# Attention with two MoE layers on one core: other places for the first tables, the first item's weights and the first loads, and a ring with two more places

## The chip, the cores and the metric

One core of a Trainium2 chip runs the whole kernel. The metric is the device time of one execution in microseconds; the times before are three executions, with their median, and one more execution was profiled. Engines are named as the profile names them: PE (TensorE matmuls), PEld (its weight loads), DVE (VectorE), ACT (ScalarE), POOL (GpSimd) and SP (SyncE, which here issues nearly all transfers). An engine works through its instructions in the order of the program; so does each queue of transfer issues.

## The reference, cut to what matters

```python
# attention: 4 batches, 12 heads, 448 tokens, head size 64, float32
scores = cap * tanh((q @ k.T / 8) / cap)
x = softmax(scores) @ v                    # becomes 1792 tokens x 768
# hard MoE: 8 experts, each 768 -> 1024 -> 768
logits = x @ w_gate + modality_bias[modality_id]
e_idx, gate = argmax(logits), softmax(logits)[e_idx]
for e in range(8):                         # tokens with e_idx == e
    y[mask] = gate[mask] * (relu(x[mask] @ w1[e]) @ w2[e])
# soft MoE: 8 experts with 4 slots each
d, c = softmax(y @ phi, axis=0), softmax(y @ phi, axis=1)
slots = d.T @ y                            # 32 slots x 768
out = c @ concat(relu(slots[e] @ m2_w1[e]) @ m2_w2[e] for e in range(8))
```

## The kernel before

**Attention** runs over 24 pairs of heads (`NPAIR`, 6 pairs a batch, numbered 0 to 23, `LAST` = 23). The loop of `attention` (lines 693 to 731) is a software pipeline written out by hand: in the round of pair p it issues the loads of pair p+2 (`load_qkv`), the scores and the tanh and exp of pair p (`scores1`, `scores2`, `scores3`), the product with V of pair p-1 (`pv`, `pv2`, and `post1`, which copies the result `o_ps` out of PSUM), the splitting of q and k of pair p+1 into a high and a low part (`split`), and the sums, turns and scaling of pair p-2 (`post2`, `post3`; `post3` ends in a write of x to `x_dram` by SP). Three places in a round, `route(p, 0)` to `route(p, 2)`, take further work from a list that `plan` fills.

**Routing** is such work. `route_batch` ranks the tokens of a batch by expert. After the third batch, `route_first` chooses the first item: a list of 4 x 117 tokens of one expert. Its parts are `f0` and `f1` (DVE), `sums_` (12 matmuls into `tab_ps`, L329, and a copy, L332), `rest` (six small DVE instructions, among them the expert's number `et_i`) and `turn` (a matmul into `tabt_ps`, L336, and four DVE instructions that give the indices `idx` and the gates `gsl`). Then `gather` (L470) fetches the 4 x 117 rows of x by indirect transfers of POOL, and `weights_first` reads the expert's number on SP and loads the first pieces of its w1 (`rw`). PSUM is lent: `Lent.tile` hands out the bank `s0` of the scores' pool, while `sums_` uses the small pool `ps_m`.

**The items.** An item is the hard MoE of up to 468 tokens of one expert: 16 pieces of w1, each split by ACT (`wh`, L810) and DVE or POOL (`wl`), then three matmul passes (L857 to L859). `item_start` (L1100) closes the attention's pools of q, k and scores, places the items' buffers and loads four tiles `w2r` (`w2load`), which the products `wphi_ps` (L834) of the first piece read. Four items run one after the other. Ahead of the first, behind the loop of pairs (lines 733 to 748), the gathered rows are scaled by their gates (`xscale`, in turn on DVE and ACT), the first two weight pieces are split (`wfirst`) and x is transposed (`xprep`).

**The soft MoE** ends the kernel. Its weights are 64 units of 768 KB (`m2_load`, L230), all loaded by SP: 32 for layer 1, then 32 for layer 2. They go through a list of places: `NRING` = 3 places of their own at first, 12 places in the attention's arena, 5 more after it, and 12 that come free behind the last item, two of them (`ring3`) closed again by `late_start` before layer 2; then places are used again (`more`). Attention loads `NRING` + 1 units, one at every second pair from pair 4 on (lines 696 to 698); the items load 16, and the rest is loaded in the last stage. The buffers `cT` and `oT` take the room of `ring3`.

**The start** (lines 1132 to 1144): the load of `cap` by ACT, a tanh that makes ACT load its table, the loads of pair 0 and `NWARM` = 5 matmuls on zeros. `early_consts` makes a scale from `cap`, `split_qk` makes the parts of q (DVE) and k (ACT casts, DVE subtracts).

Of the kernel before, what the change touches and what calls it, by code (L numbers as in the profile page):

```python
# [10 lines left out]
F32R = mybir.dt.float32r  # L11
# [41 lines left out]
def attn_moe_softmoe(ctx, tc, qT, kT, vP, cap, modality, w_gate, mod_bias, w1, w2, w2t, phi, m2_w1, m2_w2, out):  # L53
    nc = tc.nc
# [507 lines left out]
    def weights_first():  # L562
        e_first.append(load_e(NI + 3))
        for s in range(NRW):
            wload("A", s, e_first[-1])

    def attention(a1, a1q, a2p, first, ps_s, ps_o, ps_x, ps_m, item_start):
# [94 lines left out]
        extra[9] = zero_c  # L662
        class Lent:

            @staticmethod
            def tile(shape, dt, tag, name):
                n = math.prod(shape[1:])
                a = "abcd"[:len(shape) - 1]
                t = ps_s.tile([128, 512], dt, tag="s0", name=name)[:shape[0], :n]
                return t.rearrange(f"p ({' '.join(a)}) -> p {' '.join(a)}", **dict(zip(a, shape[1:])))  # L670

        todo = {}

        def plan(b):

            p, rb = (b + 1) * NP_ + 1, route_batch(b, a2p, Lent)
            at = [(p, 2), (p + 1, 1), (p + 1, 2), (p + 2, 1)]
            if b == NB1 - 1:
                f0, f1, rest, sums_, turn = route_first(a2p, ps_m, Lent)
                rb += [f0, f1, sums_, rest, lambda: (turn(), gather(NA, NB1 * S), weights_first())]  # L680
                at += [(p + 1, 2), (p + 2, 2), (p + 3, 0), (p + 3, 0), (p + 3, 1)]
                assert p + 4 == LAST
            for k, f in zip(at, rb, strict=True):
                todo.setdefault(k, []).append(f)
# [45 lines left out]
                plan((p - 2) // NP_)  # L730
            route(p, 2)
        assert not todo and n2 == NRING + 1 and a1.end <= UNIT * (NRINGA - 1)
        wsplits, xpreps = item_start()
        pv(LAST, lambda: post3(LAST - 2, a1, ps_m))
        for i in range(NT):
            xscale(NA, bool(i % 2), i)
        adds2(LAST)
# [12 lines left out]
    def load_qkv(a1, a1q, p, eng=None):  # L750
        b, hp = divmod(p, NP_)
        qr = a1q.tile([128, S], F32, tag="qr", name="qr", bufs=2)
        kr = a1q.tile([128, S + KL], F32, tag="kr", name="kr", bufs=2)
        vt = a1.tile([128, NKC + 1, 2 * HD], F32, tag="vt", name="vt", bufs=4)
        (eng or nc.sync).dma_start(kr, kT[b, hp])
        nc.sync.dma_start(qr, qT[b, hp].rearrange("h d s -> (h d) s"))
        nc.sync.dma_start(vt, vP[b, hp])
        return qr, kr, vt

# [62 lines left out]
    def w2load(j, e):  # L822
        src = w2t[bass.ds(e, 1), :, D * j:D * j + D] if j < NP2 else w2[bass.ds(e, 1), 128 * (j - NP2):128 * (j - NP2) + 128, :]
        nc.sync.dma_start(big["w2r"][j % NR2], src.rearrange("a p f -> (a p) f"))
# [269 lines left out]
    with ExitStack() as st:  # L1094
        ps_o = st.enter_context(tc.tile_pool(name="ps_o", bufs=1, space=PSUM, side="right"))
        stq = ExitStack()
        a1q = stq.enter_context(tc.tile_pool(name="a1q", bufs=1, reuse_waits="tile"))
        ps_s = stq.enter_context(tc.tile_pool(name="ps_s", bufs=1, space=PSUM))

        def item_start():  # L1100
            stq.close()
            ps_m.pools.append(stM.enter_context(tc.tile_pool(name="ps_m2", bufs=1, space=PSUM)))
            fx = stM.enter_context(tc.tile_pool(name="b_fx", bufs=1, reuse_waits="tile"))
            ps_a = stM.enter_context(tc.tile_pool(name="b_ps_a", bufs=2, space=PSUM, reuse_waits="tile"))
            ps_t = stM.enter_context(tc.tile_pool(name="b_ps_t", bufs=1, space=PSUM, reuse_waits="tile"))
            ps_l = stM.enter_context(tc.tile_pool(name="b_ps_l", bufs=1, space=PSUM, reuse_waits="tile"))
            big.update({("ps", "a"): ps_a, ("ps", "t"): ps_t, ("ps", "x"): ps_x, ("ps", "sm"): ps_m})
            big["lp"] = ps_l.tile([R, W], F32, tag="l", name="l_ps")
            fixed = fixed_in(fx)

            x0 = [fixed([128, 3, G], n, F32R) for n in ("xh0", "xl0")]
            w_at = {}
            for i in range(NWH):
                j = (HB * (TSURE + 1) - NWH + i) % NWH
                w_at[j] = [fixed([128, WC], f"{n}{j}", F32R) for n in ("wh", "wl")]
            whs.extend(w_at[i][0] for i in range(NWH))
            wls.extend(w_at[i][1] for i in range(NWH))
            x1 = [fixed([128, 3, G], n, F32R) for n in ("xh1", "xl1")]
            for n, a, b in zip(("xh", "xl"), x0, x1):
                big[n] = [t[:, k] for t in (a, b) for k in range(3)]  # L1120
            big["h"] = [fixed([128, G], f"h{i}") for i in range(NHB)]
            big["htok"] = fixed([128, NT, NF * 128], "htok")
            big["w2r"] = [fixed([128, D], f"w2r{i}") for i in range(NR2)]
            for n in ("wphi", "dhT"):
                big[n] = fixed([128, 2, 128], n)

            big["mid"] = {"dacc": big["htok"][:, NT - 1, 128 * NF - FQ:], "wacc": fixed([128, FQ], "wmid")}
            for j in range(NR2):
                w2load(j, e_first[-1])
            return [call(wfirst, s) for s in range(AHEAD)], [call(xprep, k, "aat"[k % 3]) for k in range(KD)]  # L1130

        nc.scalar.dma_start(capt, cap.partition_broadcast(128))
        nc.vector.memset(bigf, 0.0)
        nc.vector.memset(xg_all[:, 0, :256], 0.0)
        nc.scalar.activation(out=bigf, in_=bigf, func=AF.Tanh)
        first = {0: load_qkv(a1, a1q, 0, nc.gpsimd)}

        warm = ps_o.tile([128, S], F32, tag="o", name="warm")
        for _ in range(NWARM):
            nc.tensor.matmul(warm[:, :256], lhsT=xg_all[:, 0, :128], rhs=xg_all[:, 0, :256], start=True, stop=True)  # L1140
        early_consts()
        first_split = split_qk(a1q, *first[0][:2], act=True)
        first[1] = load_qkv(a1, a1q, 1)
        attention(a1, a1q, a2p, first, ps_s, ps_o, ps_x, ps_m, item_start)

# [162 lines left out]
    with ExitStack() as st:  # L1308
# [23 lines left out]
        m2_again += range(len(m2_slots) + len(r2))  # L1332
        m2_slots += r2 + r3
        NTOT = len(m2_slots)
        assert NTOT <= 4 * E
        last, freed = {s: s for s in m2_again}, {}
        for i in range(NTOT, NW):
            s = m2_again[(i - NTOT) % len(m2_again)]
# [17 lines left out]

        def late_start():

            st3.close()
            sth.close()  # L1360
            late["f"] = pool("c_ps_f", 4, space=PSUM, reuse_waits="tile")
            fixed = fixed_in(pool("c_fx2", 1, reuse_waits="tile"))
            late["cT"] = fixed([96, NTT, 128], "cT", F32R)
            late["oT"] = fixed([96, H2], "oT", F32R)

            spare.extend(m2_slots[s] for s in sorted(m2_again, key=last.get) if last[s] >= 4 * E)
            late["ct"] = [spare[0][:, NTT * NSLOT * i:NTT * NSLOT * (i + 1)].rearrange("p (t s) -> p t s", s=NSLOT)
                          for i in range(NCD)]
            late["part"] = spare[1][:, :H2]
            late["cr"] = spare[1][:, H2:H2 + 4 * 3 * NSLOT].rearrange("p (i r s) -> p i r s", r=3, s=NSLOT)  # L1370
# [34 lines left out]
        def turn(e):  # L1405
            h = hs.pop(e)
            tp = ps_t.tile([128, 2, 128], F32, tag="t", name="hT_ps")
            for i in range(2):
                nc.tensor.transpose(tp[:, i], h[:, 128 * i:128 * i + 128], ident)  # L1409
            n = NSLOT // E  # L1410
            nc.vector.tensor_copy(hT.rearrange("p (j h) s -> p h j s", h=2)[:, :, :, n * e:n * e + n],
                                  tp.rearrange("p h (j s) -> p h j s", s=NSLOT)[:, :, :, n * e:n * e + n])

        def c_load():
            for i in range(NCD):
# [69 lines left out]
        for e in range(E):  # L1485
            layer2(0, e)
            more(4 * E + 2 * e + 2)
            if e == 4:
                c_load()
        slot_out(0)  # L1490
# [20 lines left out]
        15], "pb": [6, 7, 9, 10, 12, 13, 15], "N": [6, 6, 6, 9, 9, 9, 9, 12], "comb": 6, "gath": 0, "cur": 12, "xp": [13, 13, 13], "xs": [1, 4, 4, 12], "rest": [1, 3, 7,  # L1511
        9], "pool": [4, 5]},
}
NRING = 3
NWARM = 5
NRINGA = 12
NRINGB = 5
NRING2 = 9
# [41 lines left out]
def _build(arrays):  # L1560
    import numpy as _np
    import concourse.bacc as _bacc

    nc = _bacc.Bacc("TRN2", target_bir_lowering=False, num_devices=1)
    args = []
    for name, a in arrays.items():
        args.append(nc.dram_tensor(f"in_{name}_dram", a.shape, mybir.dt.from_np(a.dtype), kind="ExternalInput").ap())
    for i, (shape, dtype) in enumerate(_OUTS):
        args.append(nc.dram_tensor(f"out_{i}_dram", shape, mybir.dt.from_np(_np.dtype(dtype)), kind="ExternalOutput").ap())
    with tile.TileContext(nc) as tc:  # L1570
        attn_moe_softmoe(tc, *args)
    return nc
# [9 lines left out]
```

## Time and profile before

| | us |
|---|---|
| median of 3 runs (501.41, 503.65, 504.35) | 503.65 |
| the profiled execution | 503.55 |
| its span, first to last instruction | 501.8 |
| PE busy | 461.4 (92%) |
| DVE busy | 291.0 (58%) |
| ACT busy | 248.7 (50%) |
| POOL busy | 66.7 (13%) |
| transfers | 124.97 MB, mean 249 GB/s |

A row of the timeline gives the start, the busy time, engine, line and operation of one instruction or of several merged ones (their count stands behind x), and in brackets the time that the engine had been idle before it, with what ended that. A row of the windows table gives, for a stretch of time, how long each engine was busy in it and with how many instructions, the clock that TensorE was granted (1.00 is 2.4 GHz, 0.50 is 1.2 GHz), the share of time in which the 16 DMA engines were busy, and what they moved. A busy PE is not a PE at its peak.

### The profile page before, as it was taken

How to read it: one execution, taken by the hardware profiler on the slowest of the kernel's cores; microseconds unless marked ns; L12 is line 12 of the kernel's file. 1: busy time of each engine (PE TensorE's matmuls, PEld its weight loads, DVE VectorE, ACT ScalarE, POOL GpSimd, SP SyncE). 2: the span in 40 equal slices, each digit the busy share in tenths (PEclk: the TensorE clock that was granted, in tenths of full speed). 3: DMA queues.
4: the chain of work that ended last, by engine and by line, in shares of the span. 5: the costliest groups of instructions: out<-in, count | busy, mean ns of one | idle time of the engine just before them, and what ended most of it. 6: DMA issues, size and time to landing. Idle time of an engine off the chain costs nothing. (4 is left out here: it accounts for less than half of the span.)

```text
span 501.8 us, 10684 instructions
## 1 busy us (share of the span) xinstructions
PE 461.4 (92%) x4077; PEld 298.2 (59%) x4077; DVE 291.0 (58%) x738; ACT 248.7 (50%) x400; POOL 66.7 (13%) x141
## 2 busy tenths in 40 slices
PE   6999999999999979899999999999999979977673
PEld 4555555555555634678876888778877845521322
DVE  3799999999999964657552546245513332001323
ACT  4988878788798748423342335334432321100312
POOL 3000000000000003013522213121013003120000
PEclk8899999999999979899999999999999999995986
DMA  6347654653353427399959997989688899999997
GB/s 187 116 93 218 197 165 118 221 158 110 126 159 104 135 82 216 99 298 325 268 183 293 319 289 242 308 287 313 206 287 320 314 418 414 414 412 415 416 414 301
DMA packets 56151, 124.97 MB, mean 249 GB/s; under 512 B 9385, under 2 KB 25456, under 8 KB 56096
## 3 DMA queue, kind: packets, MB, share of 16 engines
q1 hardware_dynamic: 53696, 117.54, 68.0%
q0 software_dynamic: 2256, 6.71, 5.0%
q8 instruction: 33, 0.54, 0.4%
q14 instruction: 22, 0.18, 0.1%
q10 hardware_dynamic: 144, 0.00, 0.0%
HBM read 112.52 MB, written 11.71 MB: 248 GB/s over the span
## 5 line engine op out<-in xcount | busy, mean ns | idle before, releaser
L608 ACT ACTIVATE arena<-arena,capb 128x1792 f32<-128x1792 f32 (+1 forms) x48 | 77.0, 1604 | 1.6
L857 PE MATMUL acc_ps<-xh,wh 128*128 128x468 f32 x192 | 75.8, 395 | 1.3 <-DVEq L1257 0.9
L107 DVE TENSOR_TENSOR arena<-arena 128x896 f32<-128x896 f32 (+1 forms) x74 | 68.0, 919 | 13.2 <-ACT arena L608 11.4
L858 PE MATMUL acc_ps<-xl,wh 128*128 128x468 f32 x192 | 71.9, 374 | 0.0
L859 PE MATMUL acc_ps<-xh,wl 128*128 128x468 f32 x192 | 71.9, 374 | 0.0
L107 DVE TENSOR_TENSOR wl<-rw,wh 128x384 fp32r<-128x384 f32 x49 | 27.3, 559 | 71.6 <-ACT wh L810 63.1
L649 PE MATMUL o_ps<-arena 128*64 128x448 f32 x288 | 61.9, 565 | 0.4 <-DVE arena L657 0.3
L810 ACT CAST wh<-rw 128x384 fp32r<-128x384 f32 x64 | 32.3, 508 | 52.1 <-PE acc_ps L858 22.5
L605 ACT ACTIVATE arena<-s_ps 128x448 f32<-128x448 f32 x96 | 46.7, 540 | 11.3 <-PE s_ps L577 11.3
L470 POOL DMA_INDIRECT xg<-x_dram,idx x16 | 16.7, 1044 | 202.2 <-PE rt_ps L520 173.4
L857 PEld LDWEIGHTS acc_ps<-xh,wh 128*128 128x128 f32 x192 | 36.3, 189 | 6.8 <-issue 1.4
L978 ACT ACTIVATE h<-acc_ps 128x468 f32<-128x468 f32 x32 | 17.9, 561 | 42.6 <-PE acc_ps L859 39.3
L859 PEld LDWEIGHTS acc_ps<-xh,wl 128*128 128x128 f32 x192 | 36.0, 188 | 5.1 <-DVE wl L107 0.5
L858 PEld LDWEIGHTS acc_ps<-xl,wh 128*128 128x128 f32 x192 | 36.4, 189 | 3.5
L649 PEld LDWEIGHTS o_ps<-arena 128*64 128x64 f32 x288 | 18.9, 140 | 30.8 <-issue 20.9
L577 PE MATMUL s_ps<-qh,kh 64*128 64x448 f32 x144 | 32.8, 443 | 2.4 <-ACT kh L765 1.9
L577 PE MATMUL s_ps<-qh,kl 64*128 64x448 f32 x144 | 27.6, 374 | 0.1
L577 PE MATMUL s_ps<-ql,kh 64*128 64x448 f32 x144 | 27.4, 371 | 0.0
L107 POOL TENSOR_TENSOR wl<-rw,wh 128x384 fp32r<-128x384 f32 x15 | 15.6, 1040 | 74.5 <-ACT wh L810 69.0
L577 PEld LDWEIGHTS s_ps<-qh,kh 64*128 64x128 f32 x144 | 14.2, 189 | 17.7 <-ACT arena L605 8.5
L600 ACT ACTIVATE arena<-sl_ps 128x448 f32<-128x448 f32 x24 | 13.0, 543 | 23.1 <-PE sl_ps L577 22.5
L906 POOL DMA_INDIRECT c_dram<-cw,icur x16 | 16.0, 1003 | 55.4 <-DVE cw L107 42.2
(271 smaller groups left out, 756.0 us busy)
## 6 DMA issues: line engine op xcount, KB each, us to landing
ring<-in_moe_w_dram SPq DMA_DIRECT2D x30, 768.0 KB
w2r<-in_moe_w2t_dram SPq DMA_DIRECT2D x32, 384.0 KB
w2r<-in_moe_w_dram SPq DMA_DIRECT2D x28, 384.0 KB
arena<-in_moe_w_dram SPq DMA_DIRECT2D x13, 768.0 KB
rw<-in_moe_w_dram SPq DMA_DIRECT2D x24, 384.0 KB
arena<-in_moe_w_dram SPq DMA_DIRECT2D x22, 384.0 KB
arena<-in_v_dram SPq DMA_DIRECT2D x24, 256.0 KB
kr<-in_k_dram SPq DMA_DIRECT2D x23, 256.0 KB
```

What stands on the lines that cost most here:

```text
L107: (eng or nc.vector).tensor_tensor(out=out, in0=in0, in1=in1, op=op)
L470: nc.gpsimd.indirect_dma_start(out=xg[:, i, :], out_offset=None, in_=x_dram if rows is None else x_dram[:rows], in_offset=bass.IndirectOff ...
L577: nc.tensor.matmul(o, lhsT=kk[r, k], rhs=qq[r], start=(t == 0), stop=(t == 2))
L605: nc.scalar.activation(out=dst[:, h], in_=ps[h], func=AF.Tanh)
L608: nc.scalar.activation(out=t, in_=t, func=AF.Exp, scale=capb)
L649: nc.tensor.matmul(o[hd], lhsT=vt[:, c, hd], rhs=pt_t[p][:, c, h] if c < 2 else pt_m[p][:, 1 + h], start=(c == 0), stop=False)
L810: nc.scalar.copy(wh, rw)
L857: nc.tensor.matmul(ps, lhsT=wh, rhs=hi[k], start=(k == 0), stop=False)
L858: nc.tensor.matmul(ps, lhsT=wh, rhs=lo[k], start=False, stop=False)
L859: nc.tensor.matmul(ps, lhsT=wl, rhs=hi[k], start=False, stop=(k == total - 1))
L906: nc.gpsimd.indirect_dma_start(out=c_dram[i % NCD], out_offset=bass.IndirectOffsetOnAxis(ap=icur[:, i:i + 1], axis=0), in_=cw[:, i, :], in ...
L978: nc.scalar.activation(out=big["h"][n % NHB], in_=acc.pop(n), func=AF.Relu)
```

## The change

It has five parts. The first ring has five places (`NRING` = 5), taken from the scratch for descriptors of POOL's transfers, which is set to 4096 bytes of each partition; attention so loads six units, and the two places of `ring3` are closed, and `cT` and `oT` placed, behind the first expert of layer 2. In `plan`, `sums_` and `rest` of the first tables go from place 0 to place 1 of pair 22 and `turn` with the gather from place 1 to place 2; the sums use the lent bank `s0`, the turn the bank `o` of the result `o_ps`. `weights_first` leaves the gather's side and is called, together with the four loads of `w2r`, inside the last pair's `pv`, behind `post3` of pair 21. The k of pair 0 is loaded by SP and no longer by POOL, its q by ACT and no longer by SP, ahead of the tanh. The warm-up has 7 matmuls and not 5.

```diff
+            def __init__(self, pool, tag, width):
+                self.where = pool, tag, width
+            def tile(self, shape, dt, tag, name):
+                pool, tag, width = self.where
...
-                t = ps_s.tile([128, 512], dt, tag="s0", name=name)[:shape[0], :n]
+                t = pool.tile([128, width], dt, tag=tag, name=name)[:shape[0], :n]
...
+        lent_s, lent_o = Lent(ps_s, "s0", 512), Lent(ps_o, "o", S)
...
-            p, rb = (b + 1) * NP_ + 1, route_batch(b, a2p, Lent)
+            p, rb = (b + 1) * NP_ + 1, route_batch(b, a2p, lent_s)
...
-                f0, f1, rest, sums_, turn = route_first(a2p, ps_m, Lent)
-                rb += [f0, f1, sums_, rest, lambda: (turn(), gather(NA, NB1 * S), weights_first())]
-                at += [(p + 1, 2), (p + 2, 2), (p + 3, 0), (p + 3, 0), (p + 3, 1)]
+                f0, f1, rest, sums_, turn = route_first(a2p, lent_s, lent_o)
+                rb += [f0, f1, sums_, rest, lambda: (turn(), gather(NA, NB1 * S))]
+                at += [(p + 1, 2), (p + 2, 2), (p + 3, 1), (p + 3, 1), (p + 3, 2)]
...
-        wsplits, xpreps = item_start()
-        pv(LAST, lambda: post3(LAST - 2, a1, ps_m))
+        wsplits, xpreps, more_weights = item_start()
+        pv(LAST, lambda: (post3(LAST - 2, a1, ps_m), weights_first(), more_weights()))
...
-        (eng or nc.sync).dma_start(kr, kT[b, hp])
-        nc.sync.dma_start(qr, qT[b, hp].rearrange("h d s -> (h d) s"))
+        nc.sync.dma_start(kr, kT[b, hp])
+        (eng or nc.sync).dma_start(qr, qT[b, hp].rearrange("h d s -> (h d) s"))
...
-            for j in range(NR2):
-                w2load(j, e_first[-1])
-            return [call(wfirst, s) for s in range(AHEAD)], [call(xprep, k, "aat"[k % 3]) for k in range(KD)]
+            return ([call(wfirst, s) for s in range(AHEAD)], [call(xprep, k, "aat"[k % 3]) for k in range(KD)],
+                    lambda: [w2load(j, e_first[-1]) for j in range(NR2)])
...
+        first = {0: load_qkv(a1, a1q, 0, nc.scalar)}
         nc.scalar.activation(out=bigf, in_=bigf, func=AF.Tanh)
-        first = {0: load_qkv(a1, a1q, 0, nc.gpsimd)}
...
-        assert NTOT <= 4 * E
+        assert NTOT <= 4 * E + 2
...
         def late_start():
-            st3.close()
             sth.close()
             late["f"] = pool("c_ps_f", 4, space=PSUM, reuse_waits="tile")
-            fixed = fixed_in(pool("c_fx2", 1, reuse_waits="tile"))
-            late["cT"] = fixed([96, NTT, 128], "cT", F32R)
-            late["oT"] = fixed([96, H2], "oT", F32R)
...
+        def last_place():
+            st3.close()
+            fixed = fixed_in(pool("c_fx2", 1, reuse_waits="tile"))
+            late["cT"] = fixed([96, NTT, 128], "cT", F32R)
+            late["oT"] = fixed([96, H2], "oT", F32R)
...
             layer2(0, e)
             more(4 * E + 2 * e + 2)
+            if e == 0:
+                last_place()
...
-NRING = 3
-NWARM = 5
+NRING = 5
+NWARM = 7
...
-    nc = _bacc.Bacc("TRN2", target_bir_lowering=False, num_devices=1)
+    nc = _bacc.Bacc("TRN2", target_bir_lowering=False, num_devices=1, dynamic_dma_scratch_size=4096)
```

## Rows read from the trace of the kernel before

**Rows 1.** Windows: us, busy per engine, PEclk, DMA share, GB/s; the tail
```profile
413.00:440.00 27.00, 26.70 (x414) 14.26 (x418) 4.97 (x28) 3.79 (x11) 7.32 (x20) 1.00 1.02 415
...
440.00:487.10 47.10, 33.97 (x276) 11.65 (x268) 9.36 (x19) 6.61 (x14) 4.98 (x30) 0.86 1.02 414
```

**Rows 2.** Timeline of SP in the tail: start us, us, engine, line, operation, count
```profile
398.66 18.31 SPq L230 DMA_DIRECT2D ring<-in_moe_w_dram  x15
```

**Rows 3.** Timeline at the end, the last layer-2 matmuls; brackets: idle before
```profile
487.13 0.85 PE L1448 MATMUL o_ps<-ring,hE 128*32 128x384 f32 x8 [0.94 <-DMA ring<-in_moe_w_dram]
```

**Rows 4.** Timeline of the start
```profile
1.39 4.16 PE L1140 MATMUL warm<-xg 128*128 128x256 f32 x10 [1.39 <-DVE xg L1134]
...
4.88 0.15 DVE L110 TENSOR_SCALAR capb<-capt 128x1 f32<-128x1 f32 x1 [3.55 <-DMA capt<-in_cap_dram]
...
6.74 0.62 ACT L765 CAST kh<-kr 128x512 fp32r<-128x512 f32 x1 [3.93 <-DMA kr<-in_k_dram]
...
7.41 0.47 PE L577 MATMUL s_ps<-qh,kh 64*128 64x448 f32 x2 [1.86 <-ACT kh L765]
...
13.85 0.98 ACT L605 ACTIVATE arena<-s_ps 128x448 f32<-128x448 f32 x2 [0.74 <-PE s_ps L577]
```

**Rows 5.** Windows, the first scores
```profile
7.40:15.60 8.20, 7.08 (x33) 4.79 (x33) 4.24 (x10) 5.83 (x8) 1.12 (x8) 0.58 0.67 195
```

**Rows 6.** Timeline: o_ps copies of two pairs, then pair 22 on DVE and PE
```profile
34.96 0.62 DVE L657 COPY arena<-o_ps 128x448 f32<-128x448 f32 x1
...
42.43 0.62 DVE L657 COPY arena<-o_ps 128x448 f32<-128x448 f32 x1
...
176.72 0.62 DVE L657 COPY arena<-o_ps 128x448 f32<-128x448 f32 x1
...
178.22 0.25 DVE L107 TENSOR_TENSOR f_tmp<-oh,esel 112x96 f32<-112x96 f32 x1
...
179.83 1.40 PE L329 MATMUL tab_ps<-bsel,a 112*32 112x117 f32 x24 [2.77 <-DVE a L107]
...
181.29 0.28 DVE L332 COPY tab<-tab_ps 128x117 f32<-128x117 f32 x1 [1.60 <-PE tab_ps L329]
...
186.88 0.33 DVE L110 TENSOR_SCALAR arena<-r_ps,gvec 128x112 f32<-128x112 f32 x1 [1.46 <-PE r_ps L507]
...
187.56 0.16 DVE L110 TENSOR_SCALAR emp<-tabt_ps 117x4 f32<-117x4 f32 x1 [0.35 <-PE tabt_ps L336]
...
189.10 0.62 DVE L657 COPY arena<-o_ps 128x448 f32<-128x448 f32 x1
...
189.71 0.37 PE L577 MATMUL s_ps<-qh,kh 64*128 64x448 f32 x2
```

**Rows 7.** Windows, PE after the tables
```profile
181.20:187.10 5.90, 5.90 (x50) 2.30 (x48) 4.21 (x13) 0.31 (x1) 0.00 (x0) 0.61 0.41 134
```

**Rows 8.** Timeline of the handover to the first item
```profile
189.09 1.16 POOL L470 DMA_INDIRECT xg<-x_dram,idx  x1 [173.37 <-PE rt_ps L520]
...
191.24 1.94 SPq L824 DMA_DIRECT2D w2r<-in_moe_w2t_dram  x4
...
193.32 1.09 POOL L470 DMA_INDIRECT xg<-x_dram,idx  x1 [0.30 <-issue]
...
201.22 0.33 SPq L528 DMA_DIRECT2D x_dram<-arena  x1
...
203.93 0.94 ACT L478 ACTIVATE xg<-xg,gsl 117x768 f32<-117x768 f32 x1 [4.27 <-DMA xg<-x_dram,idx]
...
204.77 0.91 ACT L810 CAST wh<-rw 128x384 fp32r<-128x384 f32 x2
...
211.63 1.50 PE L834 MATMUL wphi_ps<-w2r,phi_sb 128*32 128x256 f32 x24
```

**Rows 9.** Windows, the handover's loads
```profile
191.30:198.10 6.80, 6.51 (x61) 3.17 (x59) 3.06 (x4) 6.74 (x9) 2.50 (x3) 1.00 0.97 286
```

**Rows 10.** Tile xg: the gathers' time from issue to landing
```profile
DMA to landing us min/median/max: 7.7/9.3/10.6
```

More of the change, by code (lines that the diff above doesn't have):

```diff
@@ L663, in attention @@
         class Lent:
-            @staticmethod
-            def tile(shape, dt, tag, name):
+            def __init__(self, pool, tag, width):
+                self.where = pool, tag, width
+            def tile(self, shape, dt, tag, name):
+                pool, tag, width = self.where
                 n = math.prod(shape[1:])
                 a = "abcd"[:len(shape) - 1]
-                t = ps_s.tile([128, 512], dt, tag="s0", name=name)[:shape[0], :n]
+                t = pool.tile([128, width], dt, tag=tag, name=name)[:shape[0], :n]
                 return t.rearrange(f"p ({' '.join(a)}) -> p {' '.join(a)}", **dict(zip(a, shape[1:])))
+        lent_s, lent_o = Lent(ps_s, "s0", 512), Lent(ps_o, "o", S)
         todo = {}
         def plan(b):
-            p, rb = (b + 1) * NP_ + 1, route_batch(b, a2p, Lent)
+            p, rb = (b + 1) * NP_ + 1, route_batch(b, a2p, lent_s)
             at = [(p, 2), (p + 1, 1), (p + 1, 2), (p + 2, 1)]
             if b == NB1 - 1:
-                f0, f1, rest, sums_, turn = route_first(a2p, ps_m, Lent)
-                rb += [f0, f1, sums_, rest, lambda: (turn(), gather(NA, NB1 * S), weights_first())]
-                at += [(p + 1, 2), (p + 2, 2), (p + 3, 0), (p + 3, 0), (p + 3, 1)]
+                f0, f1, rest, sums_, turn = route_first(a2p, lent_s, lent_o)
+                rb += [f0, f1, sums_, rest, lambda: (turn(), gather(NA, NB1 * S))]
+                at += [(p + 1, 2), (p + 2, 2), (p + 3, 1), (p + 3, 1), (p + 3, 2)]
                 assert p + 4 == LAST
```

## The prediction

> **What bounds the kernel now.** I read the windows table over the whole span first, then the waits of PE and SP, then the timeline where a window showed an idle or slowed PE. Three stretches are not simply "PE works".
>
> The tail is the plainest. From 413 to 440 us and from 440 to 487.1 us the DMA engines are busy all the time and move 415 and 414 GB/s [rows 1]. SP issues the weight loads of the last layer pair back to back from 398.66 us on [rows 2]. PE's last layer-2 matmuls start at 487.13 us, and they waited for a `ring` load [rows 3]. So between 398.66 and 487 us the end is set by bytes over bandwidth; what follows 487.13 is a fixed chain of outputs.
>
> The second is the start. The last load that the first scores need is k, through POOL's queue; its cast waited 3.93 us for it and started at 6.74 [rows 4]. PE has been idle for 1.86 us since its warm-up matmuls ended at 5.55 [rows 4], and between 7.4 and 15.6 us its granted clock is 0.58 [rows 5], a mixture of both levels, 1.2 GHz for most of it.
>
> The third is the handover from attention to the first item. In pair 22 PE waits 2.77 us for the tables' operand `a`, and the row of `tab_ps` shows it [rows 6]. Right after it the clock is down: 0.61 on average from 181.2 to 187.1 us [rows 7]. The o_ps copies of two undisturbed pairs stand 42.43 - 34.96 = 7.47 us apart; here it is 189.10 - 176.72 = 12.38 us [rows 6]. Then the first item waits for its inputs: the scaling of the last gathered tile starts at 203.93 after 4.27 us of waiting for the gather, and the casts of the first weights only at 204.77 [rows 8]. Everything else is a PE-bound stream, which a shift passes through unchanged.
>
> **Part 1, two more places in the first ring.** Two units of 768 KB (786,432 bytes each) move from the tail into attention, which issues one unit at every second pair, now six and not four. The total of units stays 64; the last stage has 42 and not 44 left to load. At the tail's 414 GB/s that is 2 x 0.786 MB / 414 GB/s = **3.8 us** less, all on the path that sets the end, since the engines are full over the whole of it [rows 1 to 3]. The price in attention: 1.57 MB more while it lasts. They go behind the q, k, v loads of two pairs ahead (15 us of slack at 7.47 us a pair [rows 6]), so I cost them at nothing; without that cover each would hold the next loads by 0.786 MB / 414 GB/s = 1.9 us. Freeing the last two places after layer 2's first expert rather than before it delays only the allocation of `cT` and `oT`, written several experts later: nothing. The `ct` loads keep their place. I take 3.8, between 3.4 and 4.0.
>
> **Part 2, the first loads and the warm-up.** k of pair 0 goes to SP's queue as its first load, q to ACT's behind `cap`; POOL issues nothing there. Two loads of those queues bound the landing: `cap` let DVE start at 4.88 [rows 4], and q, the first load of SP, never made DVE wait. So k is there between about 4.9 and 5.5, its cast (0.62) ends by 5.5 to 6.1, and q, now behind `cap`, comes at 5.4 to 6.0. DVE then needs 1.15 us for the high and low part of q before the low part of k, which would start at 6.6 to 7.1 and not behind the cast at 6.74 + 0.62 = 7.4 [rows 4]: a gain of 0.3 to 0.8, I take 0.5. The two extra warm-up calls are four more passes at 4.16 / 10 = 0.42 us each at most [rows 4], so PE is busy until 6.4 to 7.2 and nearly meets the first scores; they cost nothing unless the k side is ready sooner than that. Without the 1.86 us hole the clock should not fall as early. What that returns is read on ACT, which is continuous from 13.85 us on: it waited 0.74 for PE there [rows 4]. I take 0.7 of a possible 0 to 0.9. Together **1.2 us**, between 0.2 and 1.9.
>
> **Part 3, the first tables.** The sums go behind the pair's PV products and post2, and the turned table from place 1 to place 2. So PE no longer stands 2.77 us in front of PV, and the stretch at half clock behind it goes. What is late next: the turn now uses the PSUM bank of `o`, so it waits for the copy of o_ps, which is behind the whole DVE queue. DVE runs from 178.22 to the end of that copy, 189.10 + 0.62 = 189.72; in between it waited 1.60, 1.46 and 0.35 us for PE, and the 0.65 us of four table instructions (0.16 each) now come behind [rows 6]. Left are 11.50 - 3.41 - 0.6 = 7.5 us of work, so the copy ends at 185.7 to 185.9. PE, at full clock, has done its 7.5 us plus 0.7 us of sums by about 184.5, so it waits 1.2 to 1.9 us here. The last pair's scores then begin near 186.2 instead of 189.71 [rows 6]: 3.5 us sooner. The tables follow on DVE, indices at 187.3 and not 188.1; PV of pair 22, which reuses the bank, is just behind them. The gather starts about 0.8 us sooner only.
>
> **Part 4, the first item's weights.** Before, four w2r loads (1.57 MB) start at 191.24, between the four gathers, the last of which POOL issues at 193.32 [rows 8]; the engines are 0.97 busy from 191.3 to 198.1 [rows 9]. Landing took 7.7 to 10.6 us [rows 10]; the last tile was late at 203.93. Now both kinds of weight load stand on SP behind the x_dram write of post3 of pair 21 (201.22 before [rows 8], 3.5 sooner = 197.7). The gathers have the engines nearly to themselves, so I take the shortest landing: 192.5 + 7.7 = 200.2, scaling 0.94, casts at 201.1 (with the median of 9.3: 202.7). The rw loads: the write's 0.23 MB and their own 0.79 MB at the 286 GB/s of that window [rows 9] take 3.6 us, so they are there at 201.3, the first half a microsecond or more sooner. Both inputs say casts 3.6 us sooner than 204.77. Against it: w2r is now in the queue behind rw, 0.23 + 0.79 + 1.57 MB from 197.7 at 286 GB/s = 9.1 us, there at 206.8, or at 208.1 if one gather (0.36 MB) still moves beside it. The products that read it stood at 211.63 [rows 8], now 208.0. That leaves a wait of 0 to 1 us; I take 0.4. Sum of parts 3 and 4: **3.2 us**, between 0 and 4.3. Queued behind the waiting SP are the item's next loads, due several pieces later.
>
> The Trainium skill, "DMA: Bandwidth & Descriptors", section "Anatomy of one DMA — SWDGE (gpsimd) path", gives a transfer issued by GpSimd about 2.0 us plus its bytes over 436 GB/s; an estimate for a gather of 117 x 3072 bytes is 2.8 us. By it the last gather would be there at 196 and only rw would count: casts 4.0 rather than 3.6 us sooner, a time 0.4 us lower. The rows, all under load, show 7.7 or more [rows 10].
>
> **Part 5, descriptor scratch.** Nothing in the trace shows it full: POOL issues the four gathers one behind the other, with 4.2 us from the first (189.09) to the last [rows 8]. I cost it at nothing; the other end is the slow rival below.
>
> Sum on the profiled execution (503.55 us, span 501.8; the median of the runs is 503.65): 503.55 - 3.8 - 1.2 - 3.2 = **495.3 us**.
>
> **Rivals.** (a) The wait at the turn takes the place of the one removed. PE stands for 1.2 to 1.9 us; the hole of 1.86 us at the start and that of 2.77 us in this pair were each followed by half clock [rows 4 to 7]. A slowed stretch as long as the present one (5.9 us at 0.61 [rows 7]) loses 0.39 x 5.9 = 2.3 us, and with it post3 of pair 21, behind which rw stands: of the 3.2 us of parts 3 and 4 some 0.9 are left, or none if the stretch is longer. Time 497.6 to 498.5. For it: the DVE sum; against it: PE is busy up to the hole. The Trainium skill, "TensorE: Matmul & The Clock Gate", Part 1, says that the gate's window runs free of the program; by that rule a hole of this size may lower the clock in one execution and not in another, and nothing here decides it. (b) The first item is starved: w2r and the next rw share the queue with ring loads, and the wait is 3 us and not 0.4: 498. (c) The change doesn't do what it says in the tail: if PE's layer 2 and not the loads ended last, 3.8 is not won, 499.1. Against it: PE waited for loads up to the last expert [rows 3]. (d) More is won: the clock stays up at the start and over the handover, casts 4.5 sooner, start 1.9: 493.3 or less. (e) Slower: with a quarter of the scratch, POOL can't put four gathers in flight and waits until one has landed. With room for one, the fourth is issued at 188.3 + 3 x 7.7 = 211.4 and lands at 219.1, not 203.9: 15 us on the path, 513.8 us, more if the later items' gathers suffer too. With room for two, it lands at 205.1 and the time is 499.8. It decides against the change below two gathers, 234 rows. The Trainium skill's page on DMA puts the rings into the scratch of 16 partitions with 16 bytes a descriptor; an estimate from it is 256 entries per engine, far above what the 468 rows of four gathers, spread over 16 engines, would need.
>
> **How the numbers follow.** Forecast (492.5 to 497.5): 0.60. (a) 0.16, (b) 0.07, (c) 0.04, (d) below 492.5 0.07, (e) 0.06 (half of it around 500). The range reaches from 491.5, where all parts give their best, to 500.0, which takes in (a), (b) and (c). A measurement can tell about 0.5%, 2.5 us, from no change: below 501.1 lie all cases but the worse half of (e) and mishaps of several parts at once: faster 0.92, same 0.04, slower 0.04.
>
> **What would show it.** Right: SP's last-stage loads start some 4 us sooner and last 3.8 us less; PE's row of `tab_ps` without a wait and pair 22's copy 8.5 to 9 us behind the last; the last scaling near 200 us; gathers landing in under 8 us. Wrong: a clock of 0.5 after the turn; wphi_ps waiting long for w2r; gathers further than 1.4 us apart on POOL; a tail window at 415 GB/s that is as long as before.

## The result and the profile after

The changed kernel takes 497.2 us in the median of six runs (496.2 to 498.5), before 504.0 (499.8 to 506.4); the ratio is 0.9888, 95% interval 0.9851 to 0.9925, so 5.6 us less. The profiled execution took 496.8 us, its span is 495.1. That is 6.7 us under the span before. The forecast was 495.3, its range 491.5 to 500.0: right as a whole, 1.9 us under the median, with a sum whose terms did not all come out.

Where the two profiled executions part, by rows that both have (after minus before):

| row | before | after | difference |
|---|---|---|---|
| copy of o_ps, pair 21 | 176.72 | 175.07 | -1.7 |
| copy of o_ps, pair 22 | 189.10 | 183.26 | -5.8 |
| first casts of w1 | 204.77 | 199.53 | -5.2 |
| first relu of the first item | 216.43 | 212.03 | -4.4 |
| relu of item 0's third block | 277.15 | 273.17 | -4.0 |
| last relu of the items | 401.55 | 397.39 | -4.2 |
| SP's first load of the last stage | 398.66 | 394.50 | -4.2 |
| last layer-2 matmuls | 487.13 | 480.62 | -6.5 |

Item 0 is the second of the four items; the first one has no number. So the attention and the handover won 5.8 us, 1.6 of them were given back up to the last relu of the items, and the tail added 2.3. The timeline of the start of the kernel after answers to [rows 4], the window to [rows 5]:

```profile
1.38 5.32 PE L1143 MATMUL warm<-xg 128*128 128x256 f32 x14 [1.38 <-DVE xg L1137]
...
5.24 0.62 ACT L769 CAST kh<-kr 128x512 fp32r<-128x512 f32 x1 [1.96 <-DMA kr<-in_k_dram]
...
6.33 0.45 DVE L110 TENSOR_SCALAR qh<-qr,qsc 128x448 fp32r<-128x448 f32 x1 [1.06 <-DMA qr<-in_q_dram]
...
7.42 0.68 DVE L107 TENSOR_TENSOR kl<-kr,kh 128x512 fp32r<-128x512 f32 x1
...
7.00:15.60 8.60, 6.64 (x43) 3.68 (x45) 5.20 (x12) 6.86 (x9) 1.25 (x9) 1.00 0.71 209
```

k is there 1.5 us sooner, but q, behind `cap` on ACT's queue and issued at 1.30 us instead of 0.92, now makes DVE wait 1.06 us, and the low part of k starts at 7.42, as late as before. What is new is the clock: 1.00 over the first scores, where the same window before has 0.60.

The handover of the kernel after, timeline, answers to [rows 6, 8]. Its last line is the time of the first item's gathers from issue to landing:

```profile
179.63 0.81 PE L329 MATMUL tab_ps<-bsel,a 112*32 112x117 f32 x24
...
183.26 0.60 DVE L657 COPY arena<-o_ps 128x448 f32<-128x448 f32 x1
...
183.92 0.39 PE L336 MATMUL tabt_ps<-fold,tab 128*117 128x32 f32 x2 [1.01 <-DVE arena L657]
...
184.24 0.47 PE L577 MATMUL s_ps<-qh,kh 64*128 64x448 f32 x2
...
191.25 1.08 POOL L470 DMA_INDIRECT xg<-x_dram,idx  x1 [0.30 <-issue]
...
195.85 0.94 ACT L478 ACTIVATE xg<-xg,gsl 117x768 f32<-117x768 f32 x1 [1.71 <-DMA xg<-x_dram,idx]
...
196.59 0.94 SPq L552 DMA_DIRECT2D rw<-in_moe_w_dram  x2
...
199.53 0.92 ACT L814 CAST wh<-rw 128x384 fp32r<-128x384 f32 x2 [2.74 <-DMA rw<-in_moe_w_dram]
...
201.71 1.72 PE L805 MATMUL xt_ps<-ident,xg 117*128 117x117 f32 x12 [2.98 <-DVE xl L107]
...
DMA to landing us min/median/max: 4.6/4.6/4.6
```

[Rows 10] is taken over the gathers of all four items. Those of the first item alone, in the kernel before:

```profile
DMA to landing us min/median/max: 9.6/10.1/10.6
```

So these gathers land some 5 us faster now that the loads of w2r are no longer among them: from the first issue to the last landing the DMA engines are busy 0.56 of the time, before 0.84. The wait for the tables' operand is gone; PE waits 1.01 us in front of the turn. The last gathered tile is there at 195.85, and now the first weights are what ends last: issued at 196.59, cast at 199.53 after a wait of 2.74. PE has a hole of 2.98 us from that. The kernel before had a smaller one in the same place:

```profile
204.91 1.12 PE L801 MATMUL xt_ps<-ident,xg 117*128 117x117 f32 x9 [2.14 <-ACT xg L478]
```

From the first casts to the first relu, windows of the kernel before and then of the kernel after (the eighth number is PEclk):

```profile
204.77:206.77 2.00, 1.85 (x11) 1.16 (x11) 1.47 (x3) 2.00 (x6) 0.00 (x0) 0.89 0.03 8
206.77:208.77 2.00, 2.00 (x11) 1.84 (x11) 1.39 (x4) 0.80 (x2) 0.00 (x0) 0.50 0.59 186
208.77:210.77 2.00, 2.00 (x11) 1.89 (x11) 1.87 (x4) 1.10 (x2) 0.00 (x0) 0.76 0.03 11
210.77:216.43 5.66, 5.66 (x76) 4.33 (x75) 1.60 (x5) 0.52 (x2) 0.99 (x1) 1.00 0.58 148
```

```profile
199.53:201.53 2.00, 0.00 (x0) 0.00 (x0) 1.46 (x3) 2.00 (x5) 0.00 (x0) 1.00 0.88 293
201.53:203.53 2.00, 1.82 (x13) 1.29 (x13) 1.81 (x5) 1.43 (x4) 0.00 (x0) 0.99 0.96 346
203.53:205.53 2.00, 1.90 (x6) 1.65 (x6) 1.97 (x7) 0.48 (x1) 0.00 (x0) 0.50 0.99 386
205.53:212.03 6.50, 6.50 (x77) 5.00 (x76) 1.00 (x3) 0.52 (x2) 1.00 (x1) 0.89 0.65 197
```

Both kernels fall to 1.2 GHz behind their hole. Before, the way from casts to relu is 216.43 - 204.77 = 11.66 us; after, where PE stands for the first 2 us of it, 12.50. So of the 5.8 us 0.6 go before the casts and 0.8 behind them. Some 0.4 us more go in item 0, where PE's wait for w2r is longer than it was before; the rows of the kernel before and of the kernel after:

```profile
274.37 0.63 PE L834 MATMUL wphi_ps<-w2r,phi_sb 128*32 128x256 f32 x6 [0.24 <-DMA w2r<-in_moe_w2t_dram]
...
269.68 1.34 PE L838 MATMUL wphi_ps<-w2r,phi_sb 128*32 128x256 f32 x12 [0.76 <-DMA w2r<-in_moe_w2t_dram]
```

That the change made this wait longer is not shown: in the profiles of all runs below PE waits there for w2r between 0 and 2.3 us in all, and 2.0 us in e8, which has the old handover.

**The tail.** The windows from SP's first load of the last stage to the update of s_acc, and from there to the last layer-2 matmuls, first of the kernel before, then of the kernel after (PEclk, DMA share and GB/s at the end of each):

```profile
398.70:412.70 14.00, 11.05 (x141) 7.25 (x139) 3.25 (x14) 3.33 (x8) 0.00 (x0) 1.00 0.93 374
412.70:487.10 74.40, 60.67 (x686) 25.91 (x686) 14.64 (x47) 10.40 (x25) 12.59 (x50) 0.91 1.02 414
```

```profile
394.50:412.60 18.10, 15.16 (x141) 8.75 (x139) 3.25 (x14) 3.34 (x8) 0.00 (x0) 0.72 0.88 347
412.60:480.60 68.00, 57.79 (x686) 25.42 (x686) 14.64 (x47) 10.43 (x25) 12.68 (x50) 0.95 1.02 414
```

The second part is 6.4 us shorter, the first 4.1 longer: the same 141 matmul records of PE at a clock of 0.72. The transfers have a hole there: SP waits for the chain's products to free the places of the next loads, 5.8 us for one of them (`q_ps`) where it waited 3.6 before, and 3.9 for another (`s_ps`) where it waited 2.0. Two windows of the kernel after show it:

```profile
404.00:406.00 2.00, 2.00 (x20) 0.59 (x12) 0.00 (x0) 0.00 (x0) 0.00 (x0) 0.50 1.01 421
406.00:408.00 2.00, 0.95 (x6) 0.49 (x10) 0.42 (x1) 0.37 (x1) 0.00 (x0) 0.50 0.63 261
408.00:410.00 2.00, 2.00 (x31) 1.21 (x27) 0.00 (x0) 0.00 (x0) 0.00 (x0) 0.50 0.82 252
```

### The profile page after: what moved, and what is told of

Same layout as the page of the kernel before. It is cut to its first block, busy times and chain, and to the rows that moved or that the text cites. A ratio compares the mean times of both kernels' runs of the same rounds, so it can differ in the third digit from the quotient of the medians.

```text
span 495.1 us, 10690 instructions
## 1 busy us (share of the span) xinstructions
PE 458.5 (93%) x4081; PEld 296.9 (60%) x4081; DVE 290.7 (59%) x738; ACT 248.7 (50%) x400; POOL 66.3 (13%) x140
## 5 line engine op out<-in xcount | busy, mean ns | idle before, releaser
L649 PE MATMUL o_ps<-arena 128*64 128x448 f32 x288 | 59.6, 548 | 0.7 <-DVE arena L657 0.6
L596 ACT ACTIVATE arena<-s_ps 128x896 f32<-128x896 f32 x24 | 21.6, 899 | 2.8 <-PE s_ps L577 2.8
```

The lines of the kernel that those rows point to most:

```text
L596: nc.scalar.activation(out=dst, in_=ps[:, :, :S], func=AF.Tanh)
L649: nc.tensor.matmul(o[hd], lhsT=vt[:, c, hd], rhs=pt_t[p][:, c, h] if c < 2 else pt_m[p][:, 1 + h], start=(c == 0), stop=False)
```

## The experiments

The theory: three gains that add up, each on its own path (bytes in the tail; the clock at the start; the order of the handover), less what PE's clock takes back in places where PE waits. The rivals: the tail is worth only the 2.3 us seen; the handover is held by gathers; the start's loads, not its clock, bring the gain; or the start's gain is swallowed later. Every ratio is to the kernel before, run beside it on the same chip.

**e1, the tail alone.** On the kernel before:

```diff
-NRING = 3
+NRING = 5
+    nc = _bacc.Bacc(..., dynamic_dma_scratch_size=4096)
...
+            if e == 0:
+                last_place()
```

> Only the two more places in the first ring, the smaller scratch and the later last place, on the kernel before. Bandwidth theory: from SP's first load of the last stage to the last layer-2 matmuls the time falls from 88.5 us to 84.7, the run is 3.8 us faster than before (ratio 0.9925), start and handover stay where they were. Rival, that PE's release of buffers sets the start of these loads and bandwidth only part of the stretch: 2.3 us, as in the whole change (ratio 0.9955). Rival, scratch too small: POOL's four gathers stand further apart than 1.4 us and the handover is later.

Measured: ratio 0.9935 (0.9898 to 0.9973), median 500.7 against 503.6. The profile settles the size; SP's first load, the last matmuls, and the two windows as above:

```profile
397.34 20.84 SPq L230 DMA_DIRECT2D ring<-in_moe_w_dram  x17
...
481.87 0.85 PE L1450 MATMUL o_ps<-ring,hE 128*32 128x384 f32 x8 [0.92 <-DMA ring<-in_moe_w_dram]
...
397.30:411.40 14.10, 11.13 (x141) 7.32 (x139) 3.29 (x16) 3.34 (x8) 0.01 (x1) 1.00 0.93 373
411.40:481.90 70.50, 57.45 (x690) 25.84 (x691) 14.63 (x47) 10.32 (x25) 12.64 (x50) 0.95 1.02 414
```

481.87 - 397.34 = 84.53 us against 88.47 before: 3.9 less, where bandwidth says 3.8, with the clock at 1.00 as before. POOL issued its four gathers within 4.25 us (188.81 to 193.06), 4.23 before: the small scratch costs nothing here. Bandwidth theory holds. The ratio alone would not tell 3.8 us from the rival's 2.3; the stretch does, and the table under e4 and e6 shows the same difference between other profiles.

**e7, one place and not two.**

```diff
-NRING = 5
+NRING = 4
-dynamic_dma_scratch_size=4096
+dynamic_dma_scratch_size=10240
```

> The changed kernel with four places in the first ring and 10240 bytes of scratch, so with one of the two units moved back into the tail. Bandwidth theory: 1.9 us slower than the change (499.1, ratio to before 0.992); the stretch from the first load of the last stage to the last layer-2 matmuls is 1.9 us longer at the same state of the clock. Rival, that the gain of the tail needs both places or comes from something else: no difference, or the whole 3.8.

Ratio 0.9941 (0.9905 to 0.9976), median 500.2. In its profile:

```profile
395.40 19.54 SPq L230 DMA_DIRECT2D ring<-in_moe_w_dram  x16
...
481.67 0.85 PE L1454 MATMUL o_ps<-ring,hE 128*32 128x384 f32 x8 [0.91 <-DMA ring<-in_moe_w_dram]
```

86.27 us, at full clock over the chain behind the last item: 88.47, 86.27 and 84.53 for three, four and five places, so about 2 us a place. By the ratios the step is 0.5% (2.7 us) against the change, and the intervals overlap.

**e2, the handover alone**: the lent banks, `plan`, `weights_first` and the loads of w2r of the change, on the kernel before.

> Only the places of the first tables, of the first item's weights and of w2r, on the kernel before. If the handover stands by itself: the copy of o_ps in pair 22 comes 8.2 us behind the one before it and not 12.4, the first weight casts 3.6 to 4.2 us sooner, 200.6 to 201.2, the run 3 to 4 us faster (ratio 0.993). If the gain needs the start's or the tail's edits: less than 1.5 us.

Ratio 0.9958 (0.9921 to 0.9996): 2.1 us, between the two expectations. In its trace the copies of pairs 21 and 22 stand 185.06 - 176.86 = 8.2 us apart, as expected; the casts come at 201.76, after 2.70 us of waiting for rw, so 3.0 us sooner than before where 3.6 to 4.2 were expected. The profiled execution is nevertheless 1.7 us slower than the one before. The items gave back 1.6 of the 3.0 us: SP's first load of the last stage is only 1.4 sooner. The chain behind the last item, at half clock for part of it, took 13.8 us (before 11.2), and SP's first load to the last matmuls 90.4, 1.9 more than before. Behind those matmuls, with the clock at 0.50 and not 0.70, another 1.2 us went. The gathers of this run, with the scratch of before, are issued 1.54, 1.40 and 2.02 us apart, those of the change 1.65, 1.41 and 1.89: the wider spacing came with the new place of the gather and not with the small scratch.

**e3, the start alone; e8, the warm-up alone; e10, the loads alone.** On the kernel before, e3 has both edits, e8 only this:

```diff
-NWARM = 5
+NWARM = 7
```

and e10 only this:

```diff
-        nc.scalar.activation(out=bigf, in_=bigf, func=AF.Tanh)
-        first = {0: load_qkv(a1, a1q, 0, nc.gpsimd)}
+        first = {0: load_qkv(a1, a1q, 0, nc.scalar)}
+        nc.scalar.activation(out=bigf, in_=bigf, func=AF.Tanh)
```

with k on SP and q on ACT in `load_qkv`.

> Only the first loads' order and queues and the two more warm-up matmuls, on the kernel before. If the clock that stays up is what counts: 1.65 us sooner by the copy of o_ps of pair 1 (25.9 instead of 27.5) and granted clock 1.00 between 7 and 15.6 us; the run 1.2 to 1.7 us faster (ratio 0.997). If a later wait swallows it: the same time as before.

> The kernel before with 7 warm-up matmuls and not 5, the loads as before. If the warm-up alone keeps the clock up: granted clock 1.00 from 7 to 15.6 us, copy of o_ps of pair 1 at 26.3 to 26.6 instead of 27.5, the first product still behind k at 7.4. If the clock needs the earlier k too: half clock from 8.3 us on as before, and 27.5.

> The kernel before with the new places of the first loads and 5 warm-up matmuls as before. The warm-up alone brought the copy of o_ps of pair 1 to 25.74. If the loads do nothing: 27.2 to 27.6, half clock from about 8 us on. If they close the hole in front of the first scores by themselves: under 27.

The copy of o_ps of pair 1 and the window of the first scores, e8:

```profile
25.74 0.62 DVE L657 COPY arena<-o_ps 128x448 f32<-128x448 f32 x1
...
7.00:15.60 8.60, 6.94 (x45) 3.85 (x46) 4.74 (x11) 6.96 (x9) 1.25 (x9) 1.00 0.64 190
```

and e10:

```profile
27.60 0.62 DVE L657 COPY arena<-o_ps 128x448 f32<-128x448 f32 x1
...
7.00:15.60 8.60, 7.21 (x33) 4.80 (x33) 4.77 (x11) 5.98 (x8) 1.25 (x9) 0.60 0.69 215
```

Before it was 27.48. The warm-up alone brings the whole 1.7 us, the loads alone nothing, in one execution of each, and the other profiles bear it out: in the nine with 7 warm-up matmuls that copy stands at 25.7 to 26.2 and the clock of the window is 1.00, in the five with 5 it stands at 27.1 to 27.6 and the clock is 0.60 to 0.65. These runs do not tell the longer warm-up from the missing hole behind it: in e8 the warm-up runs up to the first scores (7.65 us), in e10 the hole is still 1.27 us. The sooner k of e10 was undone by q, whose high part started at 6.43 and not at 5.46.

Whether the 1.7 us reach the end is not settled: e3's ratio is 1.0008 (0.9967 to 1.0048), though its profiled execution is 1.4 us shorter than the one before, while e8's only execution took 504.9 us, 1.4 more than that one. The shift is still there at the copy of pair 21, at 175.0 to 175.4 us in the nine profiles and at 176.3 to 176.9 in the five. It can be lost in the items: from the first relu to the last, where every kernel runs the same work, the fourteen profiles took 184.2 to 189.1 us (185.1 before, 185.4 after). e8 has the longest: in item 0 PE waits 2.0 us for w2r, and the clock from 265 to 285 us is 0.94 and 0.89, where it was 1.00 before. What makes this stretch vary is open; it is larger than the effect that is looked for.

**e9, the change without the start, beside e11, the change once more.**

> The changed kernel without the new first loads and with 5 warm-up matmuls, so the tail and the handover alone. If the start's 1.65 us reach the end, as a shift does that nothing swallows: 1.2 to 1.7 us slower than the changed kernel beside it. If they are swallowed later (transfers in the items, the clock), as the start alone made no difference that could be measured: the same as the changed kernel within 0.7 us.

> The changed kernel once more, beside the others of this call: ratio to before 0.985 to 0.991, 496.5 to 499; the state of the clock behind the last item may differ from the first profile.

e9: ratio 0.9900 (0.9850 to 0.9949), e11: 0.9866 (0.9817 to 0.9916). The difference of 1.7 us is what the shift should bring, but the intervals overlap widely, and in the two profiles the stretch of the items alone differs by 3.7 us (188.4 and 184.7). Together with e3 the effect lies between nothing and 1.7 us. The three parts alone (e1, e2, e3) multiply to 0.990, the change has 0.9888 and 0.9866: within the intervals they add up.

**e5, w1 of the first item sooner.** On the change:

```diff
-                rb += [f0, f1, sums_, rest, lambda: (turn(), gather(NA, NB1 * S))]
+                rb += [f0, f1, sums_, rest, lambda: (turn(), gather(NA, NB1 * S), weights_first())]
...
-        pv(LAST, lambda: (post3(LAST - 2, a1, ps_m), weights_first(), more_weights()))
+        pv(LAST, lambda: (post3(LAST - 2, a1, ps_m), more_weights()))
```

> The changed kernel with the first item's w1 loads issued right behind the gather, at place 2 of pair 22, and only w2r inside the last pair's PV. If these loads, issued behind post3 of pair 21, are now the last input of the first item: the wait of the first cast for rw (2.74 us in the change) goes, casts at about 196.8 instead of 199.5, PE's hole of 2.98 us shrinks to under 1, no half clock in the first accumulation, first relu up to 4 us sooner, the run 2 to 3.5 us faster than the change (494, ratio to before 0.981). Rival: the 0.79 MB delay the gathers instead, the last scaling moves from 195.9 to 198 and the gain is under 1 us.

Ratio 0.9812 (0.9756 to 0.9868), median 494.5: some 3 us under the change, with intervals that still overlap a little (0.9851 to 0.9925 for the change). Its timeline and a window behind it:

```profile
186.55 0.94 SPq L552 DMA_DIRECT2D rw<-in_moe_w_dram  x2
...
196.49 0.94 ACT L478 ACTIVATE xg<-xg,gsl 117x768 f32<-117x768 f32 x1 [2.58 <-DMA xg<-x_dram,idx]
...
197.33 0.91 ACT L814 CAST wh<-rw 128x384 fp32r<-128x384 f32 x2
...
202.00:204.00 2.00, 2.00 (x17) 1.38 (x19) 1.95 (x5) 0.52 (x1) 0.00 (x0) 1.00 0.76 304
```

No wait for rw is left, and the clock stays up in the first accumulation: the first relu comes at 208.34, 3.7 us sooner than in the change. Of these, 2.2 are the casts (197.33 for 199.53); the other 1.5 are the way from casts to relu, 11.01 us for 12.50, with a hole of 0.44 us and at full clock. So rw was the last input of the change. The last scaling is 0.6 us later than in the change's first profile, but in e11, without the early loads, it comes at 196.67, so a delay of the gathers by these loads is not shown.

**e12, the same loads in front of the gathers** (`lambda: (rest(), weights_first())` at place 1).

> The changed kernel with the first item's w1 loads behind the small instructions of the tables, at place 1 of pair 22, so in front of the gathers and not beside them; w2r inside the last pair's PV. Theory: the last scaling at 195.9 as in the change and not at 196.5 as with the loads beside the gathers, casts at 196.8, the run 2.5 to 3.5 us faster than the change and at most 0.5 us faster than with place 2 (493.5 to 495). Rival: SP, waiting for the expert's number, holds up the write of x and the handover gains nothing on the change.

Ratio 0.9834 (0.9795 to 0.9873), median 496.4, casts at 197.19. SP held up nothing: the write of x is issued at 184.86, in the change at 184.87. e5 and e12 can't be told apart.

**e4 and e6, small matmuls behind the last item**, in PE's waits there, on the change (17 of them) and on e5 (9):

```diff
+            nc.tensor.matmul(idle[:, :128], lhsT=ident, rhs=ident, start=True, stop=True)
...
+    busy(NFILL[0])
     dturn()
+    busy(NFILL[1])
     dispatch()
...
```

> The changed kernel with 17 small matmuls whose result nobody reads, in the waits of PE between the last item and the soft MoE. Clock theory: PE's clock stays at 2.4 GHz there, the stretch from the last relu of the items to the update of s_acc takes 11.2 us and not 15.2, the hole in the transfers 12 to 16 us behind the first load of the last stage is gone, and the run is 1.5 us faster than the change (about 495.5, ratio to before 0.985). Rival, that the clock there is not what delays the loads: the same as the change, 497.

> As the run with the early w1 loads, and 9 small matmuls whose result nobody reads in PE's waits behind the last item, few enough not to hold up the chain. Clock theory: the stretch from the last relu to the update of s_acc is 11.2 to 11.5 us in every profile, the transfers have no hole there, and another 0.5 to 1.5 us come off: 493, ratio to before 0.979. Rival, that the median execution keeps its clock there anyway: as without the matmuls.

In both profiles the clock is 1.00 from 396 to 412 us. With 17 the chain still took 12.7 us, since the first eight hold up the next step by 1.3 us; with 9 it took 11.2, as expected. The ratios are 0.9851 (0.9796 to 0.9906) and 0.9812 (0.9760 to 0.9865). e4's ratio is the one that the clock theory named and its median, 496.9, is the rival's; beside e11 (0.9866) and e5 (0.9812) no gain can be measured.

What the length of that chain does to the tail shows when all profiles are put side by side:

| places in the first ring | last relu to update of s_acc, us | SP's first load to last layer-2 matmuls, us |
|---|---|---|
| 3 | 11.2 (before, e8, e10) | 88.3 to 88.5 |
| 3 | 12.6 (e3); 13.8 (e2) | 89.2; 90.4 |
| 4 | 11.2 (e7) | 86.3 |
| 5 | 11.2 (e1, e6) | 84.5, 84.6 |
| 5 | 12.7 (e4, e5, e9, e11) | 85.4 to 85.5 |
| 5 | 13.8 (e12); 15.2 (the change) | 85.8; 86.1 |

At the shortest chain two more places are worth 3.7 to 3.9 us, in each pair of profiles; and at five places a chain that is 1.5 us longer costs the tail 0.9 us, one that is 4.1 longer costs 1.6. It is the length that counts: e4's chain ran at full clock, held up by its own matmuls, and its tail is that of the others with 12.7. So the 1.6 us that the change's first profile lacks against e1 in the tail are the price of a chain at half clock. e11, the same program, lost 0.9; what the dip costs in the median is not shown.

## Why the prediction was right, step by step

- **Part 1, 3.8 us.** The term was right: 3.9 alone (e1), about half with one place (e7). In the change's profile only 2.3 are seen, because the step "the engines are full over the whole of it" failed for 406 to 410 us: the places of the loads there are freed by the chain behind the last item, and that ran at half clock. The rows behind that step begin at 413 us; in the first 14 us of the stretch the DMA share was 0.93 before already, and what frees the places was not looked at.
- **Part 2, 1.2 us.** The size came out at 1.7 by the trace up to the end of the attention, from one term and not from two; that it lies in the range of 0.2 to 1.9 is luck. The 0.5 for the sooner k was wrong: q came at 6.3, later than the bound of 6.0, and the low part of k no sooner (e10: nothing). The 0.7 for the clock was too small, and so was its bound of 0.9: it returned 1.7 (e8). Only one wait of ACT, 0.74 us, had been counted; the activation behind it is already 1.3 us sooner in e8 (12.52 for 13.85). Whether any of it reaches the end is open.
- **Part 3.** Right in mechanism and nearly in size: the turn waits for the copy of o_ps, 1.0 us and not 1.2 to 1.9, the copy comes 8.2 us behind the last one and not 8.5 to 9, and the last pair's scores came some 3.8 us sooner (184.24 for 189.71, less the 1.7 of the start), where 3.5 were forecast.
- **Part 4.** "Casts 3.6 us sooner" beside the start's shift was right: 5.24 - 1.65 = 3.6. Both inputs were not the cause: the gathers landed in 4.6 us, far under the 7.7 taken as the shortest, and rw alone ended last, at the time worked out for it. The casts came out right all the same because the two inputs had been given nearly the same time, which is luck. The 7.7 comes from [rows 10], over all items; the first item's gathers take 9.3 to 10.6 us in the profiles with the old handover and 4.2 to 6.6 in those with the new one. The Trainium skill's estimate for a gather by "DMA: Bandwidth & Descriptors" (section "Anatomy of one DMA — SWDGE (gpsimd) path", 2.8 us) was too short, the loaded rows too long. The time of 196 that goes with it leaves out that the gather starts 0.8 us sooner (192.5 + 2.8 = 195.3); rw still ends last by it. The casts were 3.6 us sooner and not the 4.0 that the prediction drew from the estimate. The 0.4 for w2r was misplaced: there was no such wait in the first item, but 0.8 us went behind the casts, to the hole that rw left and half clock after it. Of 3.2 us, 2.5 reached the last stage in this pair of profiles.
- **"Everything else is a PE-bound stream, which a shift passes through unchanged."** This step did not hold for the items: PE waits there for w2r, and their length varies by 4.9 us between profiles. No term of the sum allowed for it.
- **Part 5.** Right: e1's gathers are as close together as before. The prediction had named gathers further than 1.4 us apart as a sign of being wrong, and in the change they are up to 1.89 apart; e2, with the full scratch, has them up to 2.02 apart, so the sign does not speak against the scratch.
- **Rivals.** (a), half clock at the turn, did not come: the clock is 1.00 there in every profile with the new handover, after a wait of 1.0 us and not 1.2 to 1.9. It came in two places that had no rival's name: behind the wait for rw, where the kernel before has it too, and behind the last item. (b), a first item starved of w2r, did not come; the waits for w2r in item 0 come with the old handover too. (c) and (e) are out by e1. (d) did not come; e5, with one more edit, is nearest to it.

## What to carry to other kernels

Where a stage is bound by bytes over bandwidth, each unit moved out of it is worth its bytes, here 3.9 us for two units where the bytes say 3.8, as long as nothing else opens a hole; so look up what frees the buffers of the first loads. When a wait is removed, look for the input that ends next, here rw behind a write of x, and move that as well: e5 has the lowest median here, 494.5 us. Where a wait of PE stays, cost it with the clock behind it, and test the clock apart from the loads. Where one stage varies by more than the gain that is looked for, compare times inside the stages over all profiles, as the table of the tail does, and not the ends of two executions.

## What was not expected of the hardware

Two matmuls more in front of the first scores kept TensorE at 2.4 GHz in all nine profiles that have them, and were worth 1.7 us up to the end of the attention, while a k that was 1.4 us sooner was worth nothing beside a q that was 1.0 later. The same chain of PE instructions behind the last item took 11.2 us in one profile of nearly the same code and 15.2 in another, where the clock was 0.50 for much of it; each us more of it cost the load-bound tail some 0.4 to 0.7. Gathers of 117 rows of 3 KB that took 9.6 to 10.6 us with the DMA engines 0.84 busy landed in 4.6 with them 0.56 busy, and in 4.9 to 5.3 beside the early loads of e5 with them 0.76 busy.
